# The first head's score operands written by ScalarE and VectorE in place of two DMAs, the raw FFN weights loaded at steps 9 and 21, and the second pair's one-hots placed first

## The chip, the core and the metric

One core of one Trainium2 chip runs the whole program. The metric is the time of one execution in microseconds (us), taken on the device; the median of three runs is given, and one further execution was recorded by the profiler. Its rows name the engines: PE (TensorE), PEld (its weight loads), ACT (ScalarE), DVE (VectorE), POOL (GpSimd) and SP (SyncE, which here only issues DMAs).

## What is computed

Clustered attention for 2 batches of 8 heads, 768 tokens and 64 channels, then a feed-forward layer with a PReLU, then a mixture of experts. The change lies in the attention:

```python
q_assign = np.argmax(np.einsum('bhsd,hcd->bhsc', q_n, c_n), axis=-1)
k_assign = np.argmax(np.einsum('bhsd,hcd->bhsc', k_n, c_n), axis=-1)
mask = q_assign[:, :, :, None] == k_assign[:, :, None, :]
scores = scale * np.matmul(q, k.transpose(0, 1, 3, 2))
scores = np.where(mask, scores, -1000000000.0)
attn = softmax(scores)              # shortened: maximum taken off, exp, divided by the sum + 1e-9
x = np.matmul(attn, v)
h = x @ w_in                        # feed-forward
y = (np.maximum(h, 0.0) + alpha * np.minimum(h, 0.0)) @ w_out
```

The mixture of experts that follows (`_moe2_ref`) takes `y`, and the change leaves it alone.

## The kernel before

**Pairs, heads, steps.** The 16 heads are worked off as 8 pairs (two heads of one batch lie on 128 partitions). A head has six blocks of 128 queries, and one block is one step: `for i in range(NI + L + 7)` counts 96 steps, 12 to a pair; in code `n` is the pair, `k` the step in it, and `m = n + 1` the pair that is being prepared meanwhile. Step 12 is the first of pair 1, step 18 the first of its second head.

**One step.** `scores` (L298) multiplies two stacked operands into PSUM: AB (q high over q low, against k high twice) and then CD (q high against k low), for two halves of 384 keys. A value is kept as a high part in a rounded format (fp32r) and a low part, the rest; the sum of the products of parts gives full precision. CD also holds, on 16 rows per head, the one-hot of the query's cluster against a mask of the key's cluster, 0 or -2^60, which does the `where`. So AB and CD together have, on 64 rows each, the tile RL: its four planes are q low, q high, k high and k low. VectorE takes the maximum (L321), ScalarE the exponential (L328); two steps later TensorE transposes the result in two groups of three (L339), ScalarE writes its high part (L341), VectorE its low part (L342), and TensorE multiplies it with v (`pv`).

**Preparing a pair.** `load` (L127) brings q and k into Tp, a single buffer, and v into `vt`. `scaleq` multiplies q by 1/8. `sims` (L181) multiplies Tp with the cluster centres: 12 products per call, then VectorE finds the maximum over the clusters, compares, and the result is weighed with `cw` so that of equal maxima the first wins; `sims2` (L203) makes the one-hot from that. For pair 0 VectorE does all of it; for later pairs POOL weighs (L201) and makes the one-hots (L216, L217). `split` (L229) lets POOL write RL, a single buffer, in two parts of four instructions: the high planes (L233), the low planes (L238). `place` (L280) copies the planes of one head from RL into AB and CD by three DMAs of 384 KB, because head 1 of a pair must change partitions and the planes are stacked; `onehots` and `placeoh` transpose the one-hots, cast them into `st` and copy them into CD by three small DMAs. AB and CD exist twice, for the even and the odd head. All these DMAs are issued on SP's queue in the order in which the program is written, and one that waits holds back those behind it.

**The start.** For pair 0 the planes of RL are written by ScalarE, VectorE and POOL (L420 to L423); `place(0, 0)` (L428) copies them. `onehot0` (L266) writes the even head's one-hots straight into CD with three ScalarE instructions for q and three for k; the odd head's go through `st` (L436 to L438). `busy` (L136) issues filler products on zeros, WARM[i] of them at a time, 14 in the last group. Steps are then driven by the tables above `attention`: ORD orders the parts of a step, SIM, SP, S2 and OK name the steps `k` at which `sims`, `split`, `sims2` and `onehots` of the next pair are issued, LK that of the load.

**The feed-forward weights.** They come as 64-bit words, are loaded raw by `Convert.load` (two DMAs of 512 KB per block, L551 and L552) and made into floats by short instructions of ScalarE, VectorE and POOL (L579 to L588). Before the feed-forward begins, three blocks are converted during attention by the generator `before()`: one small move per step (`X` in ORD) from step CV0 on, at those `k` that are not in CVX, with REST empty moves after each of the first two blocks.

Of the kernel before, what the change touches and what calls it, by code (L numbers as in the profile page):

```python
# [8 lines left out]
F32 = mybir.dt.float32  # L9
# [7 lines left out]
ALU = mybir.AluOpType  # L17
# [67 lines left out]
XG = (1, 6)  # L85
HT = 4
PACE = 7.5
CV0 = 12
LK = 8
XB = 3  # L90
LATE = 3
WARM = (8, 3, 4, 9, 14)
PREP = (33, 45)
OK = 8
CVX = (5, 6, 7, 8, 11)
REST = 4
SIM, SP, S2, VS = (1, 2), (2, 3), 3, (8, 10)
ORD = ("SMAPXaBbE", "SMAPaVBXEb", "SAPXBMabE")

# [1 line left out]
def attention(ctx, tc, A, cst, xs, Tp, conv=None, prepare=None, then=None):  # L101
# [34 lines left out]
    def busy(n):  # L136

        if n:
            w = ps_x.tile([P, 384], F32, tag="px", name="warm")
            for _ in range(n):  # L140
                nc.tensor.matmul(w, lhsT=warm[:, :P], rhs=warm[:, :384], start=True, stop=True)
# [39 lines left out]
    def sims(n, x):  # L181
        b, p = seq[n]
        if x == 0:
            pairs[n] = hk.tile([P, G, NC_], F32, tag="eq", name="eq", bufs=1)
        eq = pairs[n]
        sim = ps_t.tile([P, 512], F32, tag="pt", name="sim")
        for t in range(NT):
            nc.tensor.matmul(sim[:, t * 32:(t + 1) * 32], lhsT=Tp[:, x, t * P:(t + 1) * P],  # L188
                             rhs=bd[:, p].rearrange("p j c -> p (j c)"), start=True, stop=True)
        g = G // 2  # L190
        sv = sim[:, :g * NC_].rearrange("p (g c) -> p g c", c=NC_)
        mx = wk.tile([P, g], F32, tag="mx", name="mx")
        nc.vector.tensor_reduce(out=mx, in_=sv, axis=AX.X, op=ALU.max)
        nc.vector.tensor_tensor(out=eq[:, x * g:(x + 1) * g], in0=sv, in1=mx.unsqueeze(2).to_broadcast([P, g, NC_]), op=ALU.is_equal)
        if n == 0:
            weigh(nc.vector, eq[:, x * g:(x + 1) * g])
        elif x == 1:
            weigh(nc.gpsimd, eq)

    def weigh(eng, eq):  # L200
        eng.tensor_tensor(out=eq, in0=eq, in1=cw.unsqueeze(1).to_broadcast(eq.shape), op=ALU.mult)  # L201

    def sims2(n, xs=(0, 1)):  # L203
        eq = pairs[n]
# [61 lines left out]
    def onehot0(x):  # L266

        po = ps_t.tile([P, 512], F32, tag="pt", name="po")
        turn(hots[0], po, x)
        pv = po.rearrange("p (x g s) -> p x g s", x=2, g=2)  # L270
        for t in range(3):
            o = CDs[0][D:D + NC_].rearrange("p x (g t s) -> p x g t s", g=2, t=3)[:, x, :, t]
            i = pv[32 * t:32 * t + NC_, x]
            if x == 0:
                nc.scalar.copy(o, i)
            else:
                nc.scalar.activation(o, i, AF.Copy, bias=-BIG, scale=BIG)
        return pv
# [140 lines left out]
    es["e"] = wk.tile([P, S], F32, tag="e", name="e", bufs=3)  # L419
    nc.scalar.mul(RL[:, 1], Tp[:, 0], 0.125)  # L420
    nc.scalar.copy(RL[:, 2], Tp[:, 1])
    nc.vector.scalar_tensor_tensor(out=RL[:, 0], in0=Tp[:, 0], scalar=0.125, in1=RL[:, 1].bitcast(F32), op0=ALU.mult, op1=ALU.subtract)
    nc.gpsimd.tensor_tensor(out=RL[:, 3], in0=Tp[:, 1], in1=RL[:, 2].bitcast(F32), op=ALU.subtract)  # L423
    nc.gpsimd.memset(CDs[1][D:].bitcast(F32), 0.0)
    busy(WARM[1])
    sims(0, 0)
    sims2(0, (0,))
    place(0, 0)  # L428
    sims(0, 1)
    busy(WARM[2])  # L430
    oq = onehot0(0)
    busy(WARM[3])
    sims2(0, (1,))
    ok = onehot0(1)
    busy(WARM[4])
    st = heads[0, "st"] = hk.tile([96, 2, 2, P], F32R, tag="st", name="st", bufs=1)  # L436
    nc.vector.tensor_copy(st[:, 0], oq[:96, 0])
    nc.vector.tensor_scalar(out=st[:, 1], in0=ok[:96, 1], scalar1=BIG, scalar2=-BIG, op0=ALU.mult, op1=ALU.add)  # L438
    vsplit(0, 0)
    vsplit(0, 1)  # L440
    if len(seq) > 1:
        load(1)
        scaleq(1)
# [11 lines left out]
    for i in range(NI + L + 7):  # L455
        n, k = divmod(i, 12)
        m = n + 1
        if i == NI and then is not None:
            early.close()
            for _ in first:  # L460
                pass
            fill = then()
            next(fill)
        if conv is not None and i in (2, 3):
            conv.load(i - 2)
        if conv is not None and i == PREP[0]:
            nc.sync.dma_start(out=al, in_=A["alpha"].rearrange("(f p) -> f p", p=P))
        if conv is not None and i == PREP[1]:
            pa = ps_t.tile([P, 512], F32, tag="pt", name="pa")
            nc.tensor.transpose(pa[:, :DFF // P], al, ident[:DFF // P, :DFF // P])  # L470
            prepare(pa[:, :DFF // P])
        if i % 3 == 1 and 0 <= i - 4 < NI and (i - 4) // 3 % 4 > 1:
            recip((i - 4) // 12, (i - 4) // 3 % 2)
        gi, part = divmod(i - L - 3, 3)
        live = 0 <= gi < NI // 3
        back = 0 <= i - L < NI
        for do in ORD[i % 3]:
            if do == "S" and i < NI:
                scores(i)
            if do == "S" and k == 0 and n < len(seq):  # L480
                place(n, 1)
                placeoh(n, 1)
            if do == "M" and i < NI:
                highest(i)
            if do == "P" and live:
                pv(gi, part)
                if part == 1 and gi % 4 > 1:
                    recip2(gi // 4, gi % 2)
            if do in "AB" and back:
                transp(i - L, "AB".index(do))  # L490
            if do in "ab" and back:
                lows["ab".index(do)]()
            if do == "V" and live:
                evac(gi)
            if do == "E" and i < NI:
                expo(i)
            if do == "X" and conv is not None and CV0 <= i and (k not in CVX or i >= NI - 12):

                next(first, None)
        if live and part == 2 and gi % 4 > 1:  # L500
            late.append((i + (LATE if i < NI else 0), gi))
        if late and late[0][0] <= i:
            gl = late.pop(0)[1]
            spare += normalize(gl // 4, gl % 2)
            while spare and i < NI:
                spare.pop(0)()
        for _ in range(FILL[max(i - NI, 0)] if i >= NI else 0):
            next(fill, None)
            if spare and i > NI + NRM:
                spare.pop(0)()  # L510
        if m < len(seq):
            if k in SIM:
                sims(m, SIM.index(k))
            if k == S2 and m == 1:
                sims2(m)
            if k in SP:
                split(m, SP.index(k))
            if k == S2 and m > 1:
                sims2(m)
            if k == 6:  # L520
                place(m, 0)
            if k == (OK if m > 1 else OK - 1):
                onehots(m)
                placeoh(m, 0)
            if k == LK and m + 1 < len(seq):
                load(m + 1)
            if k == VS[0]:
                vsplit(m, 0)
            if k == VS[1]:
                vsplit(m, 1)  # L530
            if k == 11 and m + 1 < len(seq):
                scaleq(m + 1)
# [1287 lines left out]
```

## Time and profile before

| | us |
|---|---|
| median of 3 runs (lowest, highest) | 721.33 (720.0, 721.43) |
| the profiled execution | 721.68 |
| its span, first to last instruction | 719.9 |
| PE busy in the span | 701.3 |
| DVE busy | 566.4 |
| ACT busy | 471.9 |
| POOL busy | 382.3 |

A row of a timeline gives the start in the span, the duration, the engine and line, what is written from what, how many instructions were merged into the row, and in brackets how long the engine had been idle before it and what released it. The granted clock (PEclk) is 1.00 at 2.4 GHz and 0.50 at 1.2 GHz. A busy PE is a modelled figure, since its products overlap. A releaser is inferred from semaphores, and with several of them it is the one that came last.

### The profile page before, as it was taken

What the parts mean: (1) busy time and instruction counts of PE and PEld (TensorE: products, weight loads), DVE (VectorE), ACT (ScalarE), POOL (GpSimd) and SP (SyncE); (2) the same over time, 40 slices, a digit from 0 to 9 for tenths busy, and PEclk for the clock granted to TensorE, in tenths of its full rate; (3) what the DMA queues carried; (4) which work ended last, traced back from release to release, by engine and by line L of the source; (5) the groups of instructions that cost most, each with busy time, mean ns of one, the idle gap of its engine ahead of it and who ended that gap; (6) DMA issues with size and microseconds to landing.
All of it is one profiled execution on the core that took longest, in us unless ns stands there. A gap on an engine that the chain in (4) does not pass through costs nothing.

```text
span 719.9 us, 11791 instructions
## 1 busy us (share of the span) xinstructions
PE 701.3 (97%) x4119; PEld 627.2 (87%) x4119; DVE 566.4 (79%) x1112; ACT 471.9 (66%) x904; POOL 382.3 (53%) x339
## 2 busy tenths in 40 slices
PE   8999999999999999999999999999999999999995
PEld 5989999989998899888889999999888989898884
DVE  5888998799989878888884989977468888786651
ACT  5779798888889964445544655556645867574640
POOL 4539797697976486666662000001025888884201
PEclk9999999999999999999999999999999999999998
DMA  7885678656775133334303600016443998997000
GB/s 208 212 198 128 148 171 180 160 138 140 169 179 104 61 117 117 117 127 136 132 16 117 192 0 1 1 59 198 151 150 130 385 381 312 346 348 268 33 10 25
DMA packets 44128, 109.21 MB, mean 152 GB/s; under 512 B 8730, under 2 KB 24554, under 8 KB 38688
## 3 DMA queue, kind: packets, MB, share of 16 engines
q1 hardware_dynamic: 36992, 67.81, 34.6%
q0 software_dynamic: 7072, 40.60, 15.2%
q8 instruction: 34, 0.56, 0.3%
q14 instruction: 30, 0.25, 0.1%
HBM read 74.78 MB, written 10.10 MB: 118 GB/s over the span
## 4 chain that ended last, share of the span: by engine, by line
PE 67%; DMA 9%; DVE 6%; POOL 6%; ACT 5%; issue 4%; SPq 1%; POOLq 0%; ACTq 0%; DVEq 0%
PE h L671 18%; PE y L720 15%; DMA raw<-in_wall_dram,wi 6%; PE yo L1204 5%; PE pt L339 4%; PE hw L1257 4%; PE h L1204 3%; PE s L305 2%; PE px L357 2%; PE s L308 2%; PE y L730 2%; ACT e L328 2%; PE sim L188 2%; PE px L359 2%; DVE etl L342 2%
## 5 line engine op out<-in xcount | busy, mean ns | idle before, releaser
L342 DVE TENSOR_TENSOR etl<-pt,eth 128x384 fp32r<-128x384 f32 x192 | 102.1, 549 | 20.4 <-ACT eth L341 19.1
L341 ACT CAST eth<-pt 128x384 fp32r<-128x384 f32 x192 | 91.1, 486 | 21.7 <-PE pt L339 21.7
L1171 POOL DMA_INDIRECT xg<-y1d,gi x16 | 27.6, 1727 | 130.1 <-DVE gi L1020 113.8
L339 PE MATMUL pt<-ident,e 128*128 128x128 f32 x576 | 94.5, 274 | 0.3 <-ACT e L328 0.3
L321 DVE TENSOR_REDUCE nm<-s 128x1 f32<-128x768 f32 x96 | 90.4, 943 | 3.9 <-PE s L308 3.7
L328 ACT ACTIVATE e<-s,nm 128x768 f32<-128x768 f32 x96 | 87.4, 911 | 4.2 <-DVE nm L321 3.3
L699 ACT CAST gh<-gm 128x384 fp32r<-128x384 f32 x60 | 30.9, 514 | 81.7 <-DVE gm L697 58.5
L339 PEld LDWEIGHTS pt<-ident,e 128*128 128x128 f32 x576 | 74.2, 141 | 7.1 <-ACT e L328 0.6
L701 DVE TENSOR_TENSOR gl<-gm,gh 128x384 fp32r<-128x384 f32 x60 | 49.4, 823 | 25.7 <-ACT gh L699 25.7
L357 PE MATMUL px<-etl,vh 128*64 128x384 f32 (+1 forms) x192 | 65.4, 368 | 1.4 <-DVE etl L342 1.1
L305 PE MATMUL s<-AB 128*128 128x384 f32 x192 | 57.6, 381 | 2.3 <-ACT e L328 2.0
L571 POOL TENSOR_TENSOR pre<-ct,pre 128x512 int32<-128x512 int32 x26 | 37.2, 1452 | 35.8 <-DVE ct L569 35.8
L671 PE MATMUL h<-xh,wh 128*128 128x384 f32 x256 | 55.6, 338 | 0.6 <-DVE gm L694 0.4
L671 PE MATMUL h<-xh,wl 128*128 128x384 f32 x256 | 56.0, 339 | 0.0
L671 PE MATMUL h<-xl,wh 128*128 128x384 f32 x256 | 55.0, 336 | 0.0
L1539 DVE TENSOR_TENSOR wl<-raw,wh 128x2048 fp32r<-128x2048 f32 (+2 forms) x26 | 44.4, 1713 | 12.3 <-ACT wh L1535 11.0
L359 PE MATMUL px<-eth,vh 128*128 128x384 f32 x160 | 54.0, 337 | 0.0
L308 PE MATMUL s<-CD 128*128 128x384 f32 x192 | 49.7, 340 | 1.5 <-DMA CD<-st 1.0
L671 PEld LDWEIGHTS h<-xh,wh 128*128 128x128 f32 x256 | 45.5, 188 | 3.3 <-DVE gm L694 0.5
L671 PEld LDWEIGHTS h<-xh,wl 128*128 128x128 f32 x256 | 44.6, 188 | 2.7 <-POOL wl L643 2.6
L671 PEld LDWEIGHTS h<-xl,wh 128*128 128x128 f32 x256 | 45.7, 188 | 0.0
L1535 ACT CAST wh<-raw 128x2048 fp32r<-128x2048 f32 (+2 forms) x26 | 37.3, 1443 | 11.2 <-PE yo L1204 11.2
(352 smaller groups left out, 1815.3 us busy)
## 6 DMA issues: line engine op xcount, KB each, us to landing
AB<-RL SPq DMA_DIRECT2D x32, 384.0 KB, 5.2
raw<-in_w_in_dram SPq DMA_DIRECT2D x16, 512.0 KB, 4.0
raw<-in_w_out_dram SPq DMA_DIRECT2D x16, 512.0 KB, 4.7
raw<-in_wall_dram SPq DMA_DIRECT2D x8, 1024.0 KB, 7.4
Tp<-in_qkT_dram SPq DMA_DIRECT2D x16, 384.0 KB, 3.7
CD<-RL SPq DMA_DIRECT2D x16, 384.0 KB, 6.8
raw<-in_wall_dram POOLq DMA_DIRECT2D x4, 1024.0 KB
vt<-in_v_dram SPq DMA_DIRECT2D x8, 384.0 KB, 6.2
```

Source lines behind the costliest of these rows:

```text
L305: nc.tensor.matmul(s[:, u, :384], lhsT=AB[:, 0, t * P:(t + 1) * P], rhs=AB[:, 1, ks], start=True, stop=False)
L308: nc.tensor.matmul(s[:, u, :384], lhsT=CD[:, 0, t * P:(t + 1) * P], rhs=CD[:, 1, ks], start=False, stop=True)
L321: nc.vector.tensor_reduce(out=nm, in_=s[:, :, :384], axis=AX.XY, op=ALU.max, negate=True)
L328: nc.scalar.activation(e.rearrange("p (u c) -> p u c", u=2), s[:, :, :384], AF.Exp, bias=nm, accum_out=den[:, i % 3:i % 3 + 1])
L339: nc.tensor.transpose(pt[:, i2], e[:, kt * P:(kt + 1) * P], ident)
L341: nc.scalar.copy(eh, pt)
L342: lows[u] = lambda: nc.vector.tensor_tensor(out=etl[:, 3 * u:3 * u + 3, q * P:(q + 1) * P], in0=pt, in1=eh.bitcast(F32), op=ALU.subtract)
L357: nc.tensor.matmul(px[:m], lhsT=vh[:, kt, :m], rhs=etl[:, kt], start=False, stop=False)
L359: nc.tensor.matmul(px, lhsT=vh[:, kt, :], rhs=eth[:, kt], start=False, stop=(kt == NT - 1))
L671: nc.tensor.matmul(hs[c], lhsT=a[:, k * P:(k + 1) * P], rhs=x[:, k, c * HC:(c + 1) * HC], start=(k == 0 and i == 0), stop=(k == KD - 1 and ...
L720: nc.tensor.matmul(ys[gi * GT + t], lhsT=a[:, t * P:(t + 1) * P], rhs=w, start=(f == 0 and n == 0), stop=(gi == 0 and f == NF - 1 and n == 2))
L1204: nc.tensor.matmul(out, lhsT=l[:, k], rhs=r[:, k * DM:(k + 1) * DM], start=start and k == 0 and i == 0, stop=stop and k == 3 and i == len( ...
```

## The change

- Pair 0, even head: AB's upper half (q high, k high) is written from Tp by two ScalarE instructions, and the upper half of CD from RL by one VectorE copy. AB's lower half is still copied by a DMA, which now stands ahead of the fillers. `place(0, 0)` is gone.
- Of the three ScalarE instructions that write the key mask of the even head, the third is VectorE's.
- `sims` for pair 0 compares into the PSUM tile instead of into `eq`, and the weighing reads that.
- The clearing of the odd head's CD moves on POOL from ahead of the two splits of v to behind them. The last group of fillers has 6 instead of 14.
- Pair 1: `sims2` comes ahead of both parts of `split`, which are both at step 3; `onehots` and `placeoh` come at step 6, ahead of `place`.
- The raw weights of the first two blocks are loaded at steps 9 and 21 instead of 2 and 3; the conversion starts at step 16 instead of 12, with 2 empty moves after a block instead of 4.

```diff
-CV0 = 12
+RAW = (9, 21)
+CV0 = 16
...
-WARM = (8, 3, 4, 9, 14)
+WARM = (8, 3, 4, 9, 6)
...
-REST = 4
+REST = 2
...
-        nc.vector.tensor_tensor(out=eq[:, x * g:(x + 1) * g], in0=sv, in1=mx.unsqueeze(2).to_broadcast([P, g, NC_]), op=ALU.is_equal)
+        ex = eq[:, x * g:(x + 1) * g]
+        nc.vector.tensor_tensor(out=sv if n == 0 else ex, in0=sv, in1=mx.unsqueeze(2).to_broadcast([P, g, NC_]), op=ALU.is_equal)
         if n == 0:
-            weigh(nc.vector, eq[:, x * g:(x + 1) * g])
+            weigh(nc.vector, ex, sv)
         elif x == 1:
-            weigh(nc.gpsimd, eq)
+            weigh(nc.gpsimd, eq, eq)
...
                 nc.scalar.copy(o, i)
+            elif t == 2:
+                nc.vector.tensor_scalar(out=o, in0=i, scalar1=BIG, scalar2=-BIG, op0=ALU.mult, op1=ALU.add)
             else:
...
+    nc.scalar.mul(ABs[0][:D, 0], Tp[:D, 0], 0.125)
+    nc.scalar.copy(ABs[0][:D, 1], Tp[:D, 1])
     nc.vector.scalar_tensor_tensor(out=RL[:, 0], in0=Tp[:, 0], scalar=0.125, in1=RL[:, 1].bitcast(F32), op0=ALU.mult, op1=ALU.subtract)
     nc.gpsimd.tensor_tensor(out=RL[:, 3], in0=Tp[:, 1], in1=RL[:, 2].bitcast(F32), op=ALU.subtract)
-    nc.gpsimd.memset(CDs[1][D:].bitcast(F32), 0.0)
+    nc.sync.dma_start(out=ABs[0][D:].bitcast(F32), in_=RL[:D, 0:3:2].bitcast(F32))
     busy(WARM[1])
     sims(0, 0)
     sims2(0, (0,))
-    place(0, 0)
     sims(0, 1)
...
     ok = onehot0(1)
+    nc.vector.tensor_copy(CDs[0][:D], RL[:D, 1:4:2])
     busy(WARM[4])
...
     vsplit(0, 1)
+    nc.gpsimd.memset(CDs[1][D:].bitcast(F32), 0.0)
...
-        if conv is not None and i in (2, 3):
-            conv.load(i - 2)
+        if conv is not None and i in RAW:
+            conv.load(RAW.index(i))
...
             if k == S2 and m == 1:
                 sims2(m)
-            if k in SP:
+                split(m, 0)
+                split(m, 1)
+            if k in SP and m > 1:
                 split(m, SP.index(k))
             if k == S2 and m > 1:
                 sims2(m)
+            if k == (OK if m > 1 else 6):
+                onehots(m)
+                placeoh(m, 0)
             if k == 6:
                 place(m, 0)
-            if k == (OK if m > 1 else OK - 1):
-                onehots(m)
-                placeoh(m, 0)
```

In the orders below a name carries its buffer: AB0 and CD0 belong to the even heads, AB1 and CD1 to the odd ones. First SP's queue from behind the loads of pair 0, before:

```order
L283 DMA AB0_165<-RL_170 64x1536
L284 DMA AB0_165<-RL_170 64x2x768
L285 DMA CD0_166<-RL_170 64x2x768
L130 DMA Tp_91<-in_qkT_dram 128x768 x2
L132 DMA vt_267<-in_v_dram 128x2x384
L283 DMA AB1_167<-RL_170 64x1536
L284 DMA AB1_167<-RL_170 64x2x768
L285 DMA CD1_168<-RL_170 64x2x768
L290 DMA CD1_168<-st_256 16x4x128 x3
L551 DMA raw0_78<-in_w_in_dram 128x4x256
L552 DMA raw0_78<-in_w_out_dram 128x1024
L551 DMA raw1_79<-in_w_in_dram 128x4x256
```

and now:

```order
L430 DMA AB0_165<-RL_170 64x2x768
L131 DMA Tp_91<-in_qkT_dram 128x768 x2
L133 DMA vt_260<-in_v_dram 128x2x384
L287 DMA AB1_167<-RL_170 64x1536
L288 DMA AB1_167<-RL_170 64x2x768
L289 DMA CD1_168<-RL_170 64x2x768
L294 DMA CD1_168<-st_248 16x4x128 x3
L294 DMA CD0_166<-st_449 16x4x128 x3
L287 DMA AB0_165<-RL_361 64x1536
L288 DMA AB0_165<-RL_361 64x2x768
L289 DMA CD0_166<-RL_361 64x2x768
L382 DMA xb_476<-xa_475 64x384
```

One large copy instead of three stands ahead of pair 1's Tp, the raw loads are gone from here, and pair 1's one-hot copies (CD0 from st_449) stand ahead of its AB0 and CD0.

Next POOL, from the subtraction of pair 0's k on, before:

```order
L423 TENSOR_TENSOR RL_170<-Tp_91,RL_170 128x768
L424 MEMSET CD1_168 64x1536
L246 TENSOR_TENSOR vh_259<-vt_133,vh_259 128x6x64
L246 TENSOR_TENSOR vh_262<-vt_133,vh_262 128x6x64
L201 TENSOR_TENSOR eq_296<-eq_296,cw_163 128x384
L233 TENSOR_TENSOR RL_341<-Tp_91,zero_73 128x384 x4
L216 TENSOR_TENSOR eq_296<-eq_296,m2_373 128x384
L217 TENSOR_SCALAR oh_372<-eq_296 128x384
L238 TENSOR_TENSOR RL_341<-Tp_91,RL_341 128x384 x4
```

and now:

```order
L429 TENSOR_TENSOR RL_170<-Tp_91,RL_170 128x768
L248 TENSOR_TENSOR vh_251<-vt_133,vh_251 128x6x64
L248 TENSOR_TENSOR vh_254<-vt_133,vh_254 128x6x64
L447 MEMSET CD1_168 64x1536
L203 TENSOR_TENSOR eq_289<-eq_289,cw_163 128x384
L218 TENSOR_TENSOR eq_289<-eq_289,m2_357 128x384
L219 TENSOR_SCALAR oh_356<-eq_289 128x384
L235 TENSOR_TENSOR RL_361<-Tp_91,zero_73 128x384 x4
L240 TENSOR_TENSOR RL_361<-Tp_91,RL_361 128x384 x4
```

The clearing of CD1 went behind the splits of v, and the two instructions that make pair 1's one-hots went from between the parts of the split to ahead of both.

Last VectorE, from the second comparison of pair 0 to the first maxima, before:

```order
L194 TENSOR_TENSOR eq_181<-sim_200,mx_207 128x192
L201 TENSOR_TENSOR eq_181<-eq_181,cw_163 128x192
L210 TENSOR_REDUCE m2_232<-eq_181 128x12
L213 TENSOR_TENSOR oh_193<-eq_181,m2_232 128x192
L437 CAST st_256<-po_216 96x256
L438 TENSOR_SCALAR st_256<-po_235 96x256
L321 TENSOR_REDUCE nm_284<-s_270 128x1
```

and now:

```order
L196 TENSOR_TENSOR sim_199<-sim_199,mx_206 128x192
L203 TENSOR_TENSOR eq_183<-sim_199,cw_163 128x192
L212 TENSOR_REDUCE m2_231<-eq_183 128x12
L215 TENSOR_TENSOR oh_195<-eq_183,m2_231 128x192
L279 TENSOR_SCALAR CD0_166<-po_234 16x2x128
L440 COPY CD0_166<-RL_170 64x1536
L443 CAST st_248<-po_215 96x256
L444 TENSOR_SCALAR st_248<-po_234 96x256
L325 TENSOR_REDUCE nm_277<-s_263 128x1
```

The comparison stays in the PSUM tile `sim`, and a mask (L279) and a copy (L440) stand between the one-hots and the casts into `st`.

## Rows read from the trace of the kernel before

**Rows 1.** The page, busy time of the engines.

```profile
PE 701.3 (97%) x4119; PEld 627.2 (87%) x4119; DVE 566.4 (79%) x1112; ACT 471.9 (66%) x904; POOL 382.3 (53%) x339
```

**Rows 2.** Timeline of PE: start us, us, instruction, xcount [idle before <-releaser].

```profile
9.28 0.31 PE L252 MATMUL po<-identb,oh 128*96 128x128 bf16 x2 [0.97 <-DVE oh L213]
...
11.26 2.44 PE L141 MATMUL warm<-warm 128*128 128x384 bf16 x14
...
14.54 0.59 PE L308 MATMUL s<-CD 128*128 128x384 f32 x2 [0.50 <-DMA CD<-RL]
...
16.71 1.52 PE L188 MATMUL sim<-bd,Tp 128*128 128x32 f32 x12 [0.86 <-ACT Tp L222]
...
18.07 0.74 PE L305 MATMUL s<-AB 128*128 128x384 f32 x2
...
22.38 0.59 PE L305 MATMUL s<-AB 128*128 128x384 f32 x2
...
42.12 0.59 PE L308 MATMUL s<-CD 128*128 128x384 f32 x2 [0.99 <-DMA CD<-st]
```

**Rows 3.** Half-us windows: length, PE busy (x), PEclk, DMA share, GB/s.

```profile
18.00:18.50 0.50, 0.50 (x5) 0.87 0.95 166
...
21.50:22.00 0.50, 0.50 (x5) 0.72 1.22 264
```

**Rows 4.** Timeline of DVE, the first 16 us.

```profile
7.14 1.31 DVE L201 TENSOR_TENSOR eq<-eq,cw 128x192 f32<-128x192 f32 x1
...
9.92 0.36 DVE L201 TENSOR_TENSOR eq<-eq,cw 128x192 f32<-128x192 f32 x1
...
12.64 0.42 DVE L438 TENSOR_SCALAR st<-po 96x256 fp32r<-96x256 f32 x1 [1.25 <-ACT CD L277]
...
15.17 1.82 DVE L321 TENSOR_REDUCE nm<-s 128x1 f32<-128x768 f32 x2 [2.11 <-PE s L308]
```

**Rows 5.** DVE instructions by form: xcount | busy us, mean ns | idle before.

```profile
L388 DVE COPY rx<-rd 128x384 f32<-128x384 f32 x2 | 0.7, 360 | 0.1
...
L152 DVE TENSOR_SCALAR cn<-cn 128x1 f32<-128x1 f32 x1 | 0.2, 154 | 1.9 <-ACT cn L149 1.9
```

**Rows 6.** Timeline of ACT, 11 to 17 us.

```profile
11.46 1.15 ACT L277 ACTIVATE CD<-po 16x256 fp32r<-16x256 f32 x3 [0.66 <-PE po L252]
...
12.63 0.93 ACT L245 CAST vh<-vt 128x384 fp32r<-128x384 f32 x2
...
15.81 0.84 ACT L222 ACTIVATE Tp<-Tp 128x768 f32<-128x768 f32 x1 [2.26 <-DMA Tp<-in_qkT_dram]
...
16.68 0.90 ACT L328 ACTIVATE e<-s,nm 128x768 f32<-128x768 f32 x1
```

**Rows 7.** Timeline of POOL, to 82 us.

```profile
6.42 1.81 POOL L423 TENSOR_TENSOR RL<-Tp,RL 128x768 fp32r<-128x768 f32 x1 [3.07 <-ACT RL L421]
...
26.16 3.18 POOL L233 TENSOR_TENSOR RL<-Tp,zero 128x384 fp32r<-128x384 f32 x4 [1.74 <-DMA CD<-st]
...
31.75 3.92 POOL L238 TENSOR_TENSOR RL<-Tp,RL 128x384 fp32r<-128x384 f32 x4
...
53.17 3.37 POOL L233 TENSOR_TENSOR RL<-Tp,zero 128x384 fp32r<-128x384 f32 x4
...
62.79 0.75 POOL L588 TENSOR_TENSOR w32a<-raw,w32a 128x256 int32<-128x256 int32 x1
...
72.67 0.50 POOL L388 COPY rx<-rd 128x384 f32<-128x384 f32 x1
...
81.77 1.01 POOL L201 TENSOR_TENSOR eq<-eq,cw 128x384 f32<-128x384 f32 x1 [4.02 <-DMA xa<-xc]
```

**Rows 8.** Timeline of SP's queue: the loads of pair 1.

```profile
9.12 3.94 SPq L130 DMA_DIRECT2D Tp<-in_qkT_dram  x2
```

**Rows 9.** One-us windows: length, PEclk, DMA share, GB/s.

```profile
43.00:44.00 1.00, 1.00 1.01 390
...
47.00:48.00 1.00, 1.00 0.93 203
```

More of the change, by code (lines that the diff above doesn't have):

```diff
@@ L193, in sims, with weigh @@
         nc.vector.tensor_reduce(out=mx, in_=sv, axis=AX.X, op=ALU.max)
-        nc.vector.tensor_tensor(out=eq[:, x * g:(x + 1) * g], in0=sv, in1=mx.unsqueeze(2).to_broadcast([P, g, NC_]), op=ALU.is_equal)
+        ex = eq[:, x * g:(x + 1) * g]
+        nc.vector.tensor_tensor(out=sv if n == 0 else ex, in0=sv, in1=mx.unsqueeze(2).to_broadcast([P, g, NC_]), op=ALU.is_equal)
         if n == 0:
-            weigh(nc.vector, eq[:, x * g:(x + 1) * g])
+            weigh(nc.vector, ex, sv)
         elif x == 1:
-            weigh(nc.gpsimd, eq)
-    def weigh(eng, eq):
-        eng.tensor_tensor(out=eq, in0=eq, in1=cw.unsqueeze(1).to_broadcast(eq.shape), op=ALU.mult)
+            weigh(nc.gpsimd, eq, eq)
+    def weigh(eng, out, eq):
+        eng.tensor_tensor(out=out, in0=eq, in1=cw.unsqueeze(1).to_broadcast(eq.shape), op=ALU.mult)
     def sims2(n, xs=(0, 1)):
```

## The prediction, made before the changed kernel ran

> **What bounds the kernel now.** I read the page first: TensorE is busy for 97% of the span [rows 1], so the whole is a line of TensorE work, and a change that shortens nothing on TensorE can pay only where TensorE stands still, runs slowly or starts late. The change touches the first few steps, so the timeline of PE comes next, from its first real product on. It shows five places [rows 2]: TensorE waits 0.97 us for the first one-hots; then it burns 2.44 us in 14 filler products; the second half of the first score waits for the operand CD until 14.54; the similarity products of pair 1 wait 0.86 us for ScalarE's scaled Tp; and at step 12 the CD product waits 0.99 us for DMAs. The third view, windows of half a microsecond, shows the granted clock: it falls in the row from 18.0 and is back in the row from 21.5, with six rows at 0.50 (1.2 GHz) between [rows 3]. It fell after the stops just named. From step 3's AB product at 22.38 to step 12's CD product, due at 41.13 without its wait, nine steps take 18.7 us, 2.1 each [rows 2], with TensorE at work throughout, so what is gained at the start is kept as a plain shift unless a DMA or POOL is late.
>
> **Part 1: the weights of the first one-hots go through PSUM.** VectorE's first product with the cluster weights took 1.31 us, the second, of the same shape, 0.36 [rows 4]. During the first, POOL was in its subtraction until 8.23 (6.42 + 1.81) [rows 7]. Both operands of that product lay in SBUF; now one lies in PSUM, and the comparison before it, which already reads PSUM, is not slowed. That frees up to 0.95 us, but the comparison that makes the one-hots reads two SBUF operands and may now meet the same POOL instruction, which ends at 8.23. I put its end at 8.6 instead of 9.2: **0.6 us** for the first transposition. Nine fillers (2.44 / 14 = 0.174 each) follow, so the second transposition starts near 10.5 instead of 11.1.
>
> **Part 2: CD's one-hots, AB and CD written by engines.** The mask copies on ScalarE are two instead of three, 1.15 / 3 = 0.38 each [rows 6]: 10.85 to 11.6. The third is VectorE's, and it will not run beside them: the one VectorE instruction that now reads that PSUM tile started only when ScalarE's three were done (1.25 us of waiting, releaser L277) [rows 4], and the order shows a wait on ScalarE in front of the new one. So 11.65 to 12.05 (0.42 as the row of L438). Behind it on VectorE stands the copy of RL into CD, 64 x 1536. No such row exists; the nearest is a copy of 384 elements in 0.36 us, and a one-element instruction takes 0.15 [rows 5]. Fixed part taken off: 4 x 0.21 + 0.15 = 1.0 us; without a fixed part 1.44. I take 1.0, as the fixed part is seen, and keep 1.44 for the range. CD is complete at 13.05. The two ScalarE writes into AB (64 x 768) cost 0.84 each by the row of the scaling of Tp [rows 6]. ScalarE has finished RL by 6.3 (POOL waits for that and starts at 6.42 [rows 7]), so they run to 8.0, before ScalarE's next work, the one-hots, near 8.9. They cost nothing; without that gap they would cost up to 1.7. AB's other half still comes by DMA, 64 x 1536 x 4 bytes = 393 KB at 203 GB/s [rows 9], about 2 us: landed near 9.5, long before use. The 14 fillers become 6, ending near 11.9, so they are out of the way. First CD product at 13.1 instead of 14.5: **1.4 us**.
>
> **Part 3: the queue.** Before, the loads of Tp for pair 1 were issued at 9.12 behind a copy that waited for POOL [rows 8], and moved behind three copies of 393 KB. Now one such copy is ahead: it ends near 9.4, and 786 KB at 390 GB/s [rows 9] are in by about 12, not 15.8 [rows 6]. ScalarE splits v (0.93) until 12.55, scales Tp (0.84) until 13.4. VectorE has two copies for the other head (0.83) behind CD's, so its first maximum starts at 13.9 instead of 15.17 [rows 4], and the first exponential at 14.85 instead of 16.68. TensorE: scores 0 and 1 until 14.4, similarities 1.5 us until 15.9, score 2 at 15.9 instead of 18.07: **2.2 us** [rows 2, 6].
>
> **Part 4: the clock.** From score 2 to score 3 took 4.31 us [rows 2], with TensorE never idle. Of that some 3.4 us were at 1.2 GHz; at 2.4 GHz this work takes 1.7 less. The stop for Tp is gone and the one for CD is about 0.7 us. I take it that the clock stays up, and count **1.4**, a little under 1.7, because the maxima and exponentials begin to set the pace. Bounds: 0 and 1.7.
>
> **Part 5: POOL and the queue to step 12.** POOL now makes pair 1's one-hots before the splits. The two operations fill 2.4 us (26.16 + 3.18 up to 31.75) [rows 7]. Before, POOL sat idle 1.74 us ahead of the splits, until the copies out of the old RL had landed; now those land near 19 to 20, because the raw weights and two copies are out of their way, so the one-hots use that gap. With the shift of 3.6 us (2.2 + 1.4) they start somewhat before 26.16 - 3.6 = 22.6, since that start was a wait for RL. I take 22.2; the splits then run from 24.6 to 31.7 (3.18 + 3.92), against 35.67. On SP the one-hot copies now stand in front of AB and CD and wait for ScalarE's two casts after step 6, until about 29 (an estimate from the shift). Three copies of 1.94 us follow, the first near 31, the last issued at 31.7 and landed near 38. Step 12's CD product would be due at 42.12 - 0.99 - 3.6 = 37.5. About 0.6 us of waiting remains of 0.99 [rows 2]: **0.4**. Removing the raw loads from steps 2 and 3 costs nothing by itself: their first use moves from step 12 to 16.
>
> **Part 6: the raw load at step 9.** It puts 1.05 MB, 2.7 us at 390 GB/s, between Tp and the copies of head 3, whose landing frees RL for POOL's next splits. They began at 53.17, and POOL then had no gap until the copy at 72.67 that TensorE needs [rows 7]. By the same arithmetic RL is free some 0.9 us after POOL asks for it; but one conversion of 0.75 us leaves this stretch, since conversions begin four steps later. Net **-0.2**. The second load, at step 21, meets a gap of 4.02 us of POOL before its next weighing, at 81.77 [rows 7], and costs nothing. The conversion is four slots later for the first block, two for the second, none for the third, and the FFN takes them only after step 95.
>
> Sum: 2.2 + 1.4 + 0.4 - 0.2 = **3.8 us**. The profiled execution took 721.68, so 717.9. The median of the three runs is 721.33, 0.35 less, and they lie between 720.0 and 721.43: 1.4 us, as much as the clock's stretch is worth here, so one of them may have been without it. A difference of 0.2% (1.4 us) is about what can be told from none.
>
> **Rivals.** *The clock falls all the same* (20%). For: fewer fillers, and a stop before CD is left. Against: the longest stop behind the fillers, the one for Tp, is gone. Part 4 is then 0: 719.3.
>
> *VectorE's copy loses its turn to POOL* (20%). POOL's split of v starts when ScalarE's first v cast is done, near 12.2; the copy starts at 12.05. They are some 0.1 us apart. The slow 1.31 us product ended just after POOL's instruction did [rows 4, 7], so an instruction of VectorE can be held that way. If POOL is first, the copy starts after one split of 0.98 us (3.92 / 4, the same shape), or after both: CD is complete at 14.2 or 15.2, and the sum falls by 1.1 or 2.1: 719.0 or 720.0. The Trainium skill, SBUF — State Buffer, section "SBUF: two separate sides", says that VectorE and GpSimd share one pair of ports, which a VectorE instruction in a two-port mode or with two SBUF inputs, or a GpSimd instruction, holds alone until it ends. By that rule this rival is decided by which of the two starts first; the 1.31 us row agrees with the rule for two inputs, and no row here shows it for a copy.
>
> *The raw loads hit in full* (6%). Each 2.7 us lands in front of head 3's and head 5's copies, RL is late by that, POOL's unbroken chain carries it to TensorE, twice: 5.4 us against 4.0 gained by then (3.8 with part 6 taken out): 723.1, slower. For: part 6 finds RL already late. Against: the second load has 4 us of gap. It decides when RL is free more than 2 us after POOL's weighing, both times.
>
> *More is gained* (9%): step 12 no longer waits at all and RL is in time, 0.6 + 0.9 us: 716.4.
>
> The forecast itself has 45%. **Numbers.** 717.9, with 716.0 to 720.2: the better case with a little room, the clock rival, and the copy held for both splits. Faster by over 0.2% (under 719.9): 45 + 9 + most of the 40 of two rivals, 78%. Within: the held copy in its dearer form, or two rivals together, 15%. Slower: 7%.
>
> **What would show it.** First CD product at 13.1; L440 copy 1.0 us, starting at once; Tp's scaling at 12.5; score 2 at 15.9; granted clock 1.00 from 12 to 25; score 12's CD product near 38; POOL's second splits near 49.5. It is wrong if L440 stands beside an idle VectorE while POOL works, if the clock row shows 0.5, or if the offset of equal scores in the two traces shrinks after step 12.

## The result, and the profile after

The changed kernel takes 725.99 us (median of 5 runs, 724.27 to 727.58) against 721.43 (5 runs) of the kernel before beside it: ratio 1.0067, 95% interval 1.0054 to 1.0081. It is **4.6 us slower**; 3.8 us faster was forecast, and the range ended at 720.2. The profiled execution took 726.08.

The page answers to [rows 1]: TensorE is busy 0.6 us longer, in a span that is 4.4 us longer. So most of the loss is standing still.

```profile
span 724.3 us, 11778 instructions
PE 701.9 (97%) x4111; PEld 628.2 (87%) x4111; DVE 569.1 (79%) x1114; ACT 472.7 (65%) x905; POOL 384.0 (53%) x339
```

The first reading is the start of equal scores in the timeline of PE, after minus before; this difference is called the offset below. All scores of a step begin with the AB product (L309, L305 before). The rows, with the columns of [rows 2]:

```profile
5.17 5.16 PE L189 MATMUL sim<-bd,Tp 128*128 128x32 f32 x24
10.15 1.47 PE L142 MATMUL warm<-warm 128*128 128x384 bf16 x4
...
15.10 0.65 PE L309 MATMUL s<-AB 128*128 128x384 f32 x2
16.76 0.59 PE L312 MATMUL s<-CD 128*128 128x384 f32 x2 [1.00 <-DVE CD L440]
...
22.14 0.59 PE L309 MATMUL s<-AB 128*128 128x384 f32 x2
...
66.18 0.42 PE L254 MATMUL po<-identb,oh 128*96 128x128 bf16 x4 [1.86 <-POOL oh L219]
75.87 0.55 PE L401 MATMUL pb<-ident,rx 128*128 128x128 f32 x3 [1.07 <-POOL rx L392]
106.28 0.55 PE L401 MATMUL pb<-ident,rx 128*128 128x128 f32 x3 [0.63 <-POOL rx L392]
157.19 0.42 PE L254 MATMUL po<-identb,oh 128*96 128x128 bf16 x4 [0.95 <-POOL oh L219]
167.47 0.55 PE L401 MATMUL pb<-ident,rx 128*128 128x128 f32 x3 [1.80 <-POOL rx L392]
```

| step | 0 | 2 | 3 | 20 | 21 | 25 | 37 | 57 | 61 | 95 |
|---|---|---|---|---|---|---|---|---|---|---|
| after − before, us | +1.70 | +1.35 | −0.24 | −0.33 | +1.75 | +2.64 | +3.41 | +3.65 | +4.89 | +4.35 |

Two things stand there. The start was to bring 3.6 us and brought 0.24. And from step 20 on the offset grows in five jumps, each at one of the last five rows: TensorE waits 0.63 to 1.86 us, each time for POOL, be it for the one-hots (po) or for the reciprocals of the softmax sums (rx, transposed into pb). None of these waits is in the kernel before. The jumps, at steps 21, 25, 37, 57 and 61, add up to 7.0 us; between them the offset falls by 2.4, above all from step 48 on: a gain that the loss hides (e11_conv_only, below).

**The start.** The same 24 similarity products and 4 fillers took 5.16 and 1.47 us; in the trace before they take 2.79 and 0.81:

```profile
4.87 2.79 PE L188 MATMUL sim<-bd,Tp 128*128 128x32 f32 x24
7.49 0.81 PE L141 MATMUL warm<-warm 128*128 128x384 bf16 x4
```

TensorE worked at half its pace until about 13 to 14 us. Both kernels begin at that pace: the first eight fillers took 2.74 us in both, 0.34 each, where later ones take 0.17 [rows 2]. What differs is when the pace doubles, near 5 us before and near 13 after. The granted clock does not show it. It is 1.00 in these windows of PE, and also where [rows 3] had its fall:

```profile
8.00:10.00 2.00, 2.00 (x11) 1.00 0.94 197
...
18.00:19.00 1.00, 1.00 (x12) 1.00 1.06 280
```

VectorE, answering to [rows 4], did what was forecast, only later: the weighing takes 0.36 where the slow one took 1.31 (POOL's subtraction was all but over here, at 8.67; in e5_old_order it ran from 6.35 to 8.16, and the weighing at 7.55 beside it took 0.36 all the same); the mask copy waits for ScalarE's (L281); the 64 x 1536 copy takes 0.95 and starts at once.

```profile
8.61 0.36 DVE L203 TENSOR_TENSOR eq<-sim,cw 128x192 f32<-128x192 f32 x1
...
15.20 0.42 DVE L279 TENSOR_SCALAR CD<-po 16x256 fp32r<-16x256 f32 x1 [2.90 <-ACT CD L281]
15.66 0.95 DVE L440 CAST CD<-RL 64x1536 fp32r<-64x1536 f32 x1
```

ScalarE, answering to [rows 6], scales Tp at 15.97, right behind its casts of v, without the 2.26 us of waiting for the load.

**POOL and SP's queue**, answering to [rows 7] and [rows 8]. POOL, first the splits of v beside VectorE's copy, then the splits of later pairs (L235):

```profile
15.73 2.71 POOL L248 TENSOR_TENSOR vh<-vt,vh 128x384 fp32r<-128x384 f32 x2 [7.06 <-ACT vh L247]
...
51.91 1.01 POOL L203 TENSOR_TENSOR eq<-eq,cw 128x384 f32<-128x384 f32 x1 [5.39 <-DVE eq L196]
56.69 3.18 POOL L235 TENSOR_TENSOR RL<-Tp,zero 128x384 fp32r<-128x384 f32 x4 [3.77 <-DMA xa<-xc]
...
64.63 1.50 POOL L219 TENSOR_SCALAR oh<-eq 128x384 bf16<-128x384 f32 x1
...
86.35 3.18 POOL L235 TENSOR_TENSOR RL<-Tp,zero 128x384 fp32r<-128x384 f32 x4 [0.93 <-DMA CD<-st]
...
147.49 3.36 POOL L235 TENSOR_TENSOR RL<-Tp,zero 128x384 fp32r<-128x384 f32 x4 [2.23 <-DMA CD<-st]
```

The splits that began at 53.17 begin at 56.69, after 3.77 us of standing, because RL is not free: the third copy out of it (CD<-RL of the odd head) landed at 52.95 before and at 56.53 now. (The releaser xa<-xc is inferred; it is a copy that stands further back in the queue.) From there POOL has no gap: splits, one-hots at 64.63 (TensorE waits for them at 66.18), then ten instructions, the last of them the copy rx for which TensorE waits at 75.87. SP's queue shows what stands ahead:

```profile
19.90 13.93 SPq L294 DMA_DIRECT2D CD<-st  x6
...
41.53 0.47 SPq L560 DMA_DIRECT2D raw<-in_w_in_dram  x1
...
43.22 0.55 SPq L287 DMA_DIRECT2D AB<-RL  x1
...
70.91 0.47 SPq L560 DMA_DIRECT2D raw<-in_w_in_dram  x1
...
72.63 1.13 SPq L287 DMA_DIRECT2D AB<-RL  x1
...
133.15 0.53 SPq L560 DMA_DIRECT2D raw<-in_w_in_dram  x1
...
135.58 0.50 SPq L287 DMA_DIRECT2D AB<-RL  x1
```

The one-hots' DMAs hold the queue until 33.8. All three raw loads stand ahead of an odd head's copies. The third block's stood behind them before, and is now at 133.15, ahead of the copies of step 48:

```profile
109.59 0.53 SPq L551 DMA_DIRECT2D raw<-in_w_in_dram  x1
```

The windows answer to [rows 9] (length, PEclk, DMA share, GB/s; before, then after): before, the transfers end at 53, when the splits begin; after, they are at full share for two more microseconds.

```profile
52.00:53.00 1.00, 1.00 0.78 160
53.00:54.00 1.00, 1.00 0.04 8
```
```profile
54.00:55.00 1.00, 1.00 1.12 201
55.00:56.00 1.00, 1.00 0.46 88
```

### The profile page after: what moved, and what is told of

Same layout as the page of the kernel before. It is cut to its first block, busy times and chain, and to the rows that moved or that the text cites. A ratio compares the mean times of both kernels' runs of the same rounds, so it can differ in the third digit from the quotient of the medians.

```text
span 724.3 us, 11778 instructions
## 1 busy us (share of the span) xinstructions
PE 701.9 (97%) x4111; PEld 628.2 (87%) x4111; DVE 569.1 (79%) x1114; ACT 472.7 (65%) x905; POOL 384.0 (53%) x339
## 4 chain that ended last, share of the span: by engine, by line
PE 59%; DMA 13%; DVE 8%; POOL 7%; ACT 6%; issue 4%; SPq 2%; POOLq 0%; ACTq 0%; DVEq 0%
PE h L680 17%; PE y L729 14%; DMA raw<-in_wall_dram,wi 6%; PE yo L1213 5%; PE hw L1266 4%; PE h L1213 3%; PE pt L343 2%; POOL RL L240 2%; PE y L739 2%; ACT e L332 2%; DVE nm L325 2%; POOL RL L235 2%; DMA CD<-st 2%; DVE etl L346 2%; PE sim L189 2%
## 5 line engine op out<-in xcount | busy, mean ns | idle before, releaser
L309 PE MATMUL s<-AB 128*128 128x384 f32 x192 | 57.5, 381 | 1.6 <-ACT e L332 1.1
```

What stands on the lines that cost most here:

```text
L309: nc.tensor.matmul(s[:, u, :384], lhsT=AB[:, 0, t * P:(t + 1) * P], rhs=AB[:, 1, ks], start=True, stop=False)
```

## The experiments

Each time is a median and stands beside runs of the kernel before on the same chip; the ratio is to those. By the intervals, a difference between two of these runs is good to some 1.3 to 1.9 us. The names that the expectations use are the names of the runs.

### First: which part lost it

**e1_raw_only**, the raw loads and the conversion alone, in the kernel before:

```diff
-CV0 = 12
-REST = 4
+RAW, CV0, REST = (9, 21), 16, 2
-        if conv is not None and i in (2, 3):
-            conv.load(i - 2)
+        if conv is not None and i in RAW:
+            conv.load(RAW.index(i))
```

> The kernel before with only the raw loads moved to steps 9 and 21, the conversion begun at step 16 and 2 empty moves after a block. Theory A (each raw load stands in SP's queue ahead of the copies of the odd head, RL is freed late, POOL's chain reaches TensorE late): slower by 4 to 5 us, about 726, with TensorE waits on the one-hots (L217) and on rx (L388) that the kernel before does not have, at steps 21, 25, 37, 57 and 61. Theory B (the rebuilt start costs the time, the loads are harmless): 721.4, no such waits.

727.67 us, 1.0082 (1.0065 to 1.0098): 6.0 us slower, more than theory A's 4 to 5 and more than the whole change costs; B falls. TensorE waits for POOL at the five steps that A named (0.82 to 2.34 us each). POOL waits longer than in the changed kernel at the same three places, the third time 3.32 us:

```profile
55.31 3.18 POOL L234 TENSOR_TENSOR RL<-Tp,zero 128x384 fp32r<-128x384 f32 x4 [4.25 <-DMA CD<-st]
...
85.99 3.36 POOL L234 TENSOR_TENSOR RL<-Tp,zero 128x384 fp32r<-128x384 f32 x4 [1.95 <-DMA CD<-st]
```

**e2_start_only**, the changed kernel with these three settings put back (RAW (2, 3), CV0 12, REST 4).

> The changed kernel with raw loads at steps 2 and 3, conversion from step 12, 4 empty moves: everything else of the change stays. Theory A: the 4.6 us lost between steps 20 and 61 come back, so at most 721.4, and about 719.5 if the start is on average worth 2 us; no TensorE wait over 0.5 us on POOL after step 12. Theory B: 726.

722.56, 1.0011 (0.9992 to 1.0030). B falls, but A's "at most 721.4" is missed, and one wait of TensorE for POOL is left (1.07 us at 74.43). So start and order together bring nothing either. Its 12 runs lie in two groups, 719.4 to 721.2 and 723.9 to 725.8, and the profiled one (724.86) has the half-pace start. It also has POOL's wait for the copies, with no raw load near:

```profile
54.66 3.18 POOL L235 TENSOR_TENSOR RL<-Tp,zero 128x384 fp32r<-128x384 f32 x4 [1.39 <-DMA CD<-RL]
```

**e3_conv_late**, the changed kernel with RAW (2, 3) alone, conversion late.

> The changed kernel with the raw loads back at steps 2 and 3, but conversion still from step 16 with 2 empty moves, so the third block's raw load stays at step 46, ahead of the copies at step 48. Theory A: the waits at steps 21, 25 and 37 go, those at 57 and 61 (0.95 and 1.80 us) stay: some 2 us above the kernel with all of it undone. Theory C (what costs is the moved conversion work, not the transfers): as the changed kernel, 726.

723.47, 1.0015 (1.0002 to 1.0028). Theory C falls; the median is 0.9 us above e2_start_only where A wanted some 2, and as the later conversion is in it too (e11_conv_only, below), it does not price the third load. In the trace nothing is lost until step 56. Then TensorE waits 1.72 us at 154.55 and 1.82 at 164.85, behind the third load, which is issued at 129.68.

**e4_raw_2_14**, as e2_start_only with RAW (2, 14).

> As the kernel with the start alone, but the second raw load at step 14, behind the copies of the odd head in the queue. Theory A: a raw load behind those copies costs nothing: within 0.5 us of the kernel with the start alone. If any transfer in that period hurts, wherever it stands, it is slower by 1 us or more.

722.24, 1.0008 (0.9994 to 1.0021), no different from e2_start_only. That is theory A's number. But in the profiled execution, at 726.07 the slowest of its runs, POOL's splits wait 3.67 us at 56.94, though the load, issued at 52.38, stands behind the copies. So a load behind the copies is not shown to be free.

### Second: the order of pair 1 apart from the start

**e5_old_order**: e2_start_only with pair 1's order as before (the new start and nothing else).

```diff
-                split(m, 0)
-                split(m, 1)
-            if k in SP and m > 1:
+            if k in SP:
...
+            if k == 6:
+                place(m, 0)
-            if k == (OK if m > 1 else 6):
+            if k == (OK if m > 1 else OK - 1):
```

> The new start alone (raw weights, conversion and remainder as before), with the second pair's splits, placing and one-hots back in their old order. Theory O (putting the one-hots first makes SP's queue wait for ScalarE's st and so makes all three copies of the head later): score 12 starts as early against the kernel before as score 3 does, GpSimd's second halves of the splits no longer wait for CD's copy (1.39 us in e2_start_only), the wait of pb at step 25 (1.07 us) is gone, and the median falls by about 1.5 us from 722.56, to some 721. Rival Q (the order is worth nothing, the start is what varies): the median stays within 0.5 us of 722.56 and the wait at step 25 stays.

719.96, 0.9972 (0.9959 to 0.9986). The order is worth 2.6 us against e2_start_only, and theory O's signs are there. The trace, of a run of 717.51, has none of the half pace, and is the forecast's start nearly row by row:

```profile
4.97 3.09 PE L189 MATMUL sim<-bd,Tp 128*128 128x32 f32 x24
7.90 0.81 PE L142 MATMUL warm<-warm 128*128 128x384 bf16 x4
...
13.34 0.59 PE L312 MATMUL s<-CD 128*128 128x384 f32 x2 [1.10 <-DVE CD L440]
...
15.99 0.62 PE L309 MATMUL s<-AB 128*128 128x384 f32 x2
...
18.71 0.59 PE L309 MATMUL s<-AB 128*128 128x384 f32 x2
```

First CD product at 13.34 (forecast 13.1), score 2 at 15.99 (15.9), score 3 3.67 us earlier than before (3.6), and step 12 no longer waits.

**e6_warm14**: e5_old_order with the last filler group at 14 again. **e8_warm0_14**: that, with 14 fillers in place of 8 in the first group.

> As e5_old_order, with 14 fillers in place of 6 ahead of the first score. Theory W (fewer fillers let the clock fall or leave it low in some of the runs, which is what spreads them from 719.4 to 725.8): the spread of the runs shrinks to that of the kernel before (some 3.5 us) and the median is 718.5 to 720. Rival X (the slow start comes from the first 5 us, which all these kernels share): no change of the spread, first score at 15 us or later in the trace, and the 8 fillers cost up to 1.3 us where they push the first score: 721 to 722.5.

> As e6_warm14, with 14 fillers in place of 8 ahead of the centroids' transpose. Theory E (TensorE's slow products up to 14 us in the profiled runs come of too little work in the first 5 us): the products of sim take about 276 ns of the trace in place of 401, the first score starts by 13.5 us although the transpose comes up to 1 us later, and the runs lie in one hump at 718 to 720. Rival X (the slow start is not of TensorE's load at all): products of sim at 401 ns all the same, and the time is 1 us above e6_warm14.

719.17, 0.9974 (0.9962 to 0.9986), and 720.43, 0.9981 (0.9971 to 0.9990). The profiled run of e6_warm14 has the half pace (24 products in 5.20 us), that of e8_warm0_14 has not (2.80), but its runs still spread from 718.12 to 723.29. W's numbers were met, but e5_old_order had met them without the fillers (spread 3.7 us, 0.9972), and a run with 14 fillers still started at half pace. E's quick products came, but not its single group of runs, and the first score came at 15.29 instead of 13.5. Its time, 1.3 us above e6_warm14, is as rival X had it. One reason for its late first score stands in its trace: VectorE's subtraction (L428) began at 6.68, 0.07 us behind POOL's, and took 2.58 us instead of 0.96. So neither number of fillers is shown to decide which start a run gets.

**e7_order_only**: the kernel before with pair 1's new order alone (the diff of e5_old_order the other way round).

> The kernel before with nothing but the second pair's new order (both splits at step 3, one-hots ahead of the placing at step 6). Theory O: score 12 waits for CD longer than the 0.99 us of before, GpSimd's second halves wait more than 1 us for CD's copy where they waited for nothing, and the time is 722.5 to 724 against 721.6. Rival P (the prediction's part 5): 0.4 us faster, 721.2, with 0.6 us of the 0.99 us wait left.

723.09, 1.0027 (1.0013 to 1.0041): the order alone costs 2.0 us. SP's queue, POOL's splits and TensorE show how:

```profile
32.15 1.87 SPq L290 DMA_DIRECT2D CD<-st  x3
34.12 0.54 SPq L283 DMA_DIRECT2D AB<-RL  x1
```
```profile
55.85 3.18 POOL L233 TENSOR_TENSOR RL<-Tp,zero 128x384 fp32r<-128x384 f32 x4 [1.81 <-DMA CD<-RL]
```
```profile
42.90 0.62 PE L308 MATMUL s<-CD 128*128 128x384 f32 x2 [1.81 <-DMA CD<-RL]
...
75.61 0.55 PE L397 MATMUL pb<-ident,rx 128*128 128x128 f32 x3 [1.06 <-POOL rx L388]
```

AB's first copy is issued at 34.12, where it was at 29.37:

```profile
29.37 0.52 SPq L283 DMA_DIRECT2D AB<-RL  x1
```

Step 12 waits 1.81 us instead of 0.99, and RL is free 1.81 us late. The offset grows by 0.9 us at step 12 and by 1.6 between steps 20 and 25. That the even head's late copies push the odd head's is likely, but the order does not decide it alone: e3_conv_late has the new order and RL in time, e8_warm0_14 the old one and RL 1.25 us late at 53.02.

### Third: the loads apart from each other and from the conversion

All four are e6_warm14 with one thing more. Where the third load is held back, the code is:

```diff
-                conv.load(f + 2)
+                pend.append(f + 2)
...
+        if pend and 2 <= k <= 5:
+            conv.load(pend.pop(0))
```

**e9_raw_old_order** (RAW (9, 21), CV0 16, REST 2), **e10_third_quiet** (that, third load held back), **e11_conv_only** (CV0 16, REST 2, third load held back, RAW (2, 3)), **e12_splits_only** (both halves of pair 1's splits at step 3, one-hots behind the copies).

> e6_warm14 (new start, old order of the second pair) with the change's raw loads at steps 9 and 21 and its conversion (CV0 16, REST 2). Theory A (the raw loads stand ahead of the copies of an odd head in SP's queue, the copies land late, GpSimd's splits wait for them and TensorE later waits for GpSimd): some 6 us above e6_warm14, 725, with GpSimd's second splits waiting 2 to 4 us at some 54, 86 and 147 us. Rival M (what the order and the raw loads cost is one and the same lateness, paid once): 722 to 723, with waits under 1.5 us.

> As e9_raw_old_order, but the third block's raw load is held back from step 48, where it stands ahead of an odd head's copies, to step 50, behind them. Theory T (the third load alone costs what was lost at steps 57 and 61, some 3 us in e1_raw_only): 2 to 3 us less than e9_raw_old_order, no wait over 0.5 us of po or pb after 140 us. Rival B (behind the copies it slows them as much, because all share the 16 DMA engines): within 0.7 us of e9_raw_old_order.

> e6_warm14 with the change's later conversion (CV0 16, REST 2) alone: the first two raw loads stay at steps 2 and 3 and the third goes out at step 50. Theory N (the conversion's shift itself costs nothing, as the prediction had it; only loads cost): 719.2, within 0.5 us of e6_warm14, no new wait of TensorE over 0.5 us. Rival V (the conversion's pieces on ScalarE, VectorE and GpSimd fall on busier steps): 1 us or more above e6_warm14.

> e6_warm14 with one half of the second pair's new order: both halves of its splits at step 3, but placing ahead of the one-hots as before. Theory Q (what costs is SP's queue, which stands behind the one-hots' wait for ScalarE): within 0.5 us of e6_warm14, 719.2, and AB's first copy goes out by 31 us where the one-hots come first (then at 34 us). Rival H (what costs is that GpSimd does both halves in one piece after its weighing, so that the first copy has to wait anyway): 1.5 to 2.5 us above, 721 to 721.7, and the wait of GpSimd's next second split for CD's copy is over 1 us.

| run | us | ratio (95%) |
|---|---|---|
| e9_raw_old_order | 725.38 | 1.0050 (1.0032 to 1.0067) |
| e10_third_quiet | 721.90 | 1.0013 (0.9994 to 1.0033) |
| e11_conv_only | 716.66 | 0.9935 (0.9917 to 0.9952) |
| e12_splits_only | 719.91 | 0.9978 (0.9965 to 0.9990) |

Theory A holds in the sum: 6.2 us above e6_warm14, with waits of POOL of 3.36, 0.64 and 3.59 us where it had 2 to 4 each, so that the second misses; M falls. Theory T holds: holding back the third load gives 3.5 us (2.7 by the ratios, where T wanted 2 to 3), and the waits for po and pb after 140 us are gone; B falls. The first two loads cost 721.90 − 716.66 = 5.2 us; in the two traces the offset from step 16 to step 95, behind the start, differs by 5.35. The trace of e10_third_quiet shows both, POOL and then TensorE:

```profile
55.28 3.18 POOL L235 TENSOR_TENSOR RL<-Tp,zero 128x384 fp32r<-128x384 f32 x4 [3.88 <-DMA CD<-st]
...
86.15 3.37 POOL L235 TENSOR_TENSOR RL<-Tp,zero 128x384 fp32r<-128x384 f32 x4 [2.10 <-DMA CD<-st]
```
```profile
64.81 0.42 PE L254 MATMUL po<-identb,oh 128*96 128x128 bf16 x4 [2.00 <-POOL oh L219]
74.47 0.55 PE L401 MATMUL pb<-ident,rx 128*128 128x128 f32 x3 [1.07 <-POOL rx L392]
106.15 0.55 PE L401 MATMUL pb<-ident,rx 128*128 128x128 f32 x3 [1.80 <-POOL rx L392]
```

For e11_conv_only both theories fell: the later conversion is not free, it **gains**, 2.5 us against e6_warm14. From step 16 to step 94 the offset against before goes from −3.59 to −4.97 in e11_conv_only and from −1.27 to −0.51 in e6_warm14, so the gain, 2.1 us there, lies in the attention and not in the start. The offset falls by 0.3 to 0.5 us at each of the steps 48, 53 and 62 in all six traces with the later conversion, the changed kernel's among them, and in none of the other seven. A piece of the conversion (L595, 0.74 us) that stands in POOL's chain behind the one-hots in e5_old_order is gone, but that is not the gain: in e6_warm14 none of TensorE's waits above 0.15 us from step 16 to step 95 is for POOL. Which waits it saved was not separated. This version beats both kernels.

e12_splits_only speaks for theory Q: 0.7 us above e6_warm14 (0.3 by the ratios) where H wanted 1.5 to 2.5, AB's first copy issued at 31.36, and POOL's next splits wait 0.56 us where H wanted over 1. What costs in the new order is mainly the one-hots' place ahead of the copies, not the splits' place.

## Why the prediction was wrong, point by point

| part | forecast, us | measured, us | from |
|---|---|---|---|
| start (1 to 4) | −3.6 | −2.0 | e5_old_order, ratio |
| order of pair 1 (5) | −0.4 | +2.0 | e7_order_only, ratio |
| raw loads and conversion (6) | +0.2 | +6.0 | e1_raw_only |
| of it: loads at steps 9 and 21 | +0.9 | +5.2 | e10_third_quiet − e11_conv_only |
| of it: third load | 0 | +3.5 | e9_raw_old_order − e10_third_quiet |
| of it: conversion later | −0.75 | −2.5 | e11_conv_only − e6_warm14 |

The three of part 6 are steps from e6_warm14 to e9_raw_old_order and so add up to their difference, 6.2; measured on the old start it was 6.0. By the ratios the three are +5.6, +2.7 and −2.8. All parts add up to 6.0, and the change costs 4.6: order and loads make the same copies late, so part of their price may be paid only once. e9_raw_old_order, which differs from the changed kernel by the order and eight fillers, points that way (1.0050 against 1.0067, some 1.2 us for the order instead of 2.0), but the intervals overlap.

**Part 6 is the step that failed.** "RL free some 0.9 us after POOL asks for it" was 3.77 in the changed kernel, 4.25 in e1_raw_only, 3.36 in e9_raw_old_order and 3.88 in e10_third_quiet. The prediction does not show how it came from 2.7 us of load to 0.9; it takes some 1.8 us of room between the copies' landing and POOL's asking. There was none: before, the last copy landed at 52.95 and the splits started at 53.17. "The second load meets a gap of 4.02 us and costs nothing" took idle time of POOL ahead of its *weighing* for slack of RL. The weighing waits for VectorE's comparison; the splits behind it waited 0.64 to 2.10 us in the four traces, and in three of them, not in e9_raw_old_order, TensorE waits at 106 us. The rival of the raw loads had both mechanism and price: 5.4 us for two loads, 5.2 measured. Its own sign, RL over 2 us late both times, is met in e10_third_quiet alone: the second wait was 0.93 us in the changed kernel and 1.95 in e1_raw_only. Its 6% rested on that misread gap.

**A load that was not looked at.** "None for the third" was worked out for the conversion's slots only. The third block's raw load is issued where the first block's conversion ends, and so it moved from 109.59 to 133.15, ahead of an odd head's copies, and costs 3.5 us.

**Part 5** had the wrong sign. Its dates on the queue were near, given the start that this run had: the last even copy was to be issued at 31.7 with 3.4 us more of start gained, and left at 35.29. But 0.6 us of step 12's wait was to be left, and it was 1.14 in the changed kernel; with the old order the new start removed it altogether (e5_old_order). And it left out who is behind step 12: RL and POOL's chain, 1.6 us more in e7_order_only. That run keeps the raw loads at steps 2 and 3, which part 5 counted as gone, so its 2.0 is not a test of part 5 as it stood.

**Parts 1 to 4** held as mechanisms (e5_old_order, above). The clock did not fall at 18 to 22 us in any trace with the new start. But their worth is 2.0 and not 3.6: the trace of e5_old_order, of its quickest execution (717.51), has all of it, and that of e6_warm14, of one of its longest (721.25), has the half pace up to 14 us and is even with the kernel before at step 3. That this is what parts the runs is likely from such single traces, not shown. The 1.4 of part 4 is no fixed sum either: e1_raw_only has the start of the kernel before, and its trace, without the fall at 18 us, is at step 3 already 1.85 us ahead. The rival *the clock falls all the same* had the size about right, 1.4, in another place.

**The copy's turn.** VectorE's copy began at 15.66, POOL's split at 15.73: the copy took 0.95, and the two splits 2.71, against 1.97 for the same two in e7_order_only, where no such copy is:

```profile
13.26 1.97 POOL L246 TENSOR_TENSOR vh<-vt,vh 128x384 fp32r<-128x384 f32 x2 [3.61 <-issue]
```

So POOL waited and the rival did not come about. By the Trainium skill, SBUF — State Buffer, section "SBUF: two separate sides", VectorE and GpSimd share a pair of ports, and whichever starts first, a VectorE instruction in a two-port mode or with two SBUF inputs or a GpSimd one, holds it until its instruction ends. These rows agree, if this copy with one input is such an instruction: the one that was first by 0.07 us was not slowed, and the other was. The rows of e8_warm0_14 agree the other way round: there POOL's subtraction was first by 0.07 us and took 1.84 us, and VectorE's, with two SBUF inputs, took 2.58 instead of 0.96.

## What to carry to other kernels

A load's place in a queue is priced by the landing of the transfers behind it and by who waits for the buffer that they read; an idle engine near by is not slack unless the thing it waits for is that landing. When a table shifts one step, list every DMA whose place hangs on it, to the end of the program, and see what stands right behind each. Parts of one change are worth trying alone: here one of them, the later conversion, gains 2.5 us on top of the new start, and was hidden under loads that cost 8.7.

## What was not expected of the hardware

TensorE's pace in the first 14 us is not the program's alone. The program is the same up to the similarity products in e5_old_order and e6_warm14, and they took 3.09 and 5.20 us, with a granted clock of 1.00 in both. Of 11 traces with the new start 8 have the long form, two neither this nor a fall of the granted clock (e5_old_order, e8_warm0_14), and e11_conv_only has the short form and a fall at 8 to 12. The three traces with the old start have the short form and a fall later: at 18 to 22 us in the kernel before and in e7_order_only, at 8 to 12 in e1_raw_only, here the last (a window with busy time of all engines, then PEclk, DMA share, GB/s):

```profile
10.00:12.00 2.00, 2.00 (x8) 0.99 (x7) 1.13 (x4) 0.72 (x2) 0.00 (x0) 0.50 0.95 197
```

A stretch at half pace shows in the durations of equal products even where the column says 1.00. What decides which start a run gets stays open.
